# A fused DFT and GEGLU kernel: value matmuls in two accumulating passes, channel 128 through DRAM, last output pieces over all banks

## The chip, the cores and the metric

The kernel runs on one core of a Trainium2 chip. The metric is device time in microseconds (us), measured over repeated executions. Before: 684.08 us, median of 4 runs (683.23 to 684.66).

Engines: PE is the tensor engine, PEld its weight loads (they bring in the stationary operand, the matrix that stays in PE while the other streams past; they overlap its matmuls), DVE is VectorE, ACT is ScalarE, POOL is GpSimd, SP issues DMAs.

## The reference, cut to what matters

```python
X = np.fft.fft(np.fft.fft(x, axis=1), axis=2).real   # x: 8 x 3008 x 256
g   = X @ w_gate                                     # 256 x 1536
val = X @ w_val                                      # 256 x 1536
out = (gelu(g) * val) @ w_out                        # 1536 x 256, all tokens
```

## The kernel before

The real part of the DFT is symmetric, so the kernel computes half the tokens of each batch entry and splits them into an even part E and an odd part O. A token then has the gate `E@WE + O@WO` (the plus row) and its mirror token `E@WE - O@WO` (the minus row). One batch entry is a *block*, its tokens are three *chunks* of 512, 512 and 481 columns, and each chunk has twelve *units* of 128 hidden columns: 36 units a block, 288 in all. Into the units of a block the DFT of the next block is woven as filler, one small piece a unit: first eight stage-1 steps (every other unit, 16 units long), then channel steps and the E, channel-128 and O steps. The order of instructions is set by a scheduler from these pieces, not by the loop alone.

The gate takes three matmuls: E and O add up in a bank, ScalarE takes the gelu of the plus row, then M = -2·O is added to the same bank for the minus row. The value came in two forms. In 207 units ("apart") E and O were multiplied into two banks and VectorE made both rows; in 81 units a third value matmul (M) made the minus row, as for the gate, and VectorE only multiplied.

```python
def l1_value(ci, fc):                      # before, cut
    if apart(ci, fc):                      # fc % 4 != 3, and not the first chunk of block 0
        mm(pv, n, "v", "E", fs, E, True, True)
        mm(po, n, "v", "M", fs, O, True, True)
        # three VectorE passes: E + channel 128, then plus row, then minus row
        nc.vector.scalar_tensor_tensor(ve, EB_bufs[b][...], w128[...], pv, op0=ALU.mult, op1=ALU.add)
        nc.vector.scalar_tensor_tensor(vv[:, 0, :n], po, -0.5, ve, op0=ALU.mult, op1=ALU.add)
        nc.vector.scalar_tensor_tensor(<vv, reversed>, po, 0.5, ve, op0=ALU.mult, op1=ALU.add)
    else:
        mm(pv, n, "v", "E", fs, E, True, False)
        mm(pv, n, "v", "O", fs, O, False, True)
        nc.vector.tensor_tensor(h[:, fc, 0, :n], gl[:, 0, :n], pv, op=ALU.mult)   # pass 1 of 2
# l1_value2: apart -> GpSimd multiplies both rows of 1024 columns;
#            else  -> matmul with M, and VectorE's pass 2 of 2
...
def s1_pack(j0):                           # one stage-1 step
    s1_mm(j0)                              # two banks: lo, hi
    nc.scalar.activation(up8, hi, AF.Copy)
    for g, op in enumerate((ALU.add, ALU.subtract)):
        nc.vector.tensor_tensor(dst_g, lo, up8, op=op)       # two VectorE passes of 384
...
def b_pack(gi):                            # channel 128 on all partitions
    for off, k2, n in cols[gi]:            # 8 matmuls, one column of Z repeated 128 times
        nc.tensor.matmul(ps[:, off:off+n], _sub(Z, [[0, 128]], k2*C + 128), TPI[:, 0:n], ...)
    nc.scalar.activation(EB[...], ps[:, :n], AF.Copy)
```

PSUM, the memory that PE writes its sums into, has eight banks: two for the gate, three for the value, one for the output, two for the transforms.

## Time and profile before

| what | before |
|---|---|
| time | 684.08 us |
| PE / DVE / ACT / POOL busy | 652.0 / 580.4 / 484.7 / 459.9 of 681.9 us |
| period of a steady block | 79.08 us |
| block 0, from its first unit | 82.87 us |

I take stage times from the trace as the start of the weight load of each unit's WvE matrix (288 of them); a block is from its first such load to that of the next block. Only differences between kernels are read from them.

First the page of the kernel before: busy time, share of the span and instructions of each engine, then the chain of waits by engine, then three groups of instructions (busy us, mean ns of one, idle time before and what ended it).

```profile
PE 652.0 (96%) x5257; PEld 443.7 (65%) x5313; DVE 580.4 (85%) x958; ACT 484.7 (71%) x943; POOL 459.9 (67%) x264
...
PE 81%; DVE 2%; ACT 2%; issue 1%; POOL 1%; DMA 1%; SPq 0%; ACTq 0%; DVEq 0%
...
L543 DVE SCALAR_TENSOR_TENSOR ve_sb<-EB_sb,w,ps_v 128x512 f32<-128x512 bf16 (+1 forms) x207 | 150.5, 732 | 46.0 <-PE ps_v L510 45.6
L549 DVE SCALAR_TENSOR_TENSOR v_sb<-ps_v,ve_sb 128x512 f32<-128x512 f32 (+1 forms) x207 | 138.7, 670 | 0.0
L555 DVE TENSOR_TENSOR h_sb<-gelu_sb,ps_v 128x512 bf16<-128x512 bf16 (+1 forms) x81 | 54.5, 674 | 9.6 <-PE ps_v L510 7.6
```

PE is the limit over the whole span. But an average hides stages. The windows view of the kernel before gives for each stretch its length and then the busy time of each engine: the first chunk of block 0; the VectorE-heavy stretch after it; the stage-1 stretch of block 5 (its first 16 units); the rest of that block. They are cut at the WvE loads. (The prediction quotes windows cut up to 3 us later: in 434.5 to 470 VectorE is busy for 35.0 of 35.5 us.)

```profile
core 0: us, PE busy (x) PEld busy (x) DVE busy (x) ACT busy (x) POOL busy (x), PEclk, DMA share, GB/s
32.20:56.40 24.20, 24.04 (x168) 12.34 (x170) 22.40 (x36) 20.60 (x40) 0.00 (x0) 1.00 0.74 145
56.40:85.00 28.60, 28.13 (x211) 17.96 (x214) 27.99 (x50) 20.02 (x39) 16.55 (x9) 1.00 0.17 34
431.60:466.20 34.60, 34.33 (x271) 23.64 (x275) 33.73 (x58) 23.34 (x47) 23.48 (x12) 1.00 0.17 39
466.20:510.60 44.40, 44.29 (x385) 30.80 (x386) 35.98 (x58) 35.76 (x70) 33.10 (x17) 1.00 0.19 42
```

In the stage-1 stretch VectorE has almost no room left (33.73 of 34.60); after it there are eight free microseconds (35.98 of 44.40).

What one VectorE pass costs is read from starts, not from durations, since listed durations overlap. The timeline of VectorE before (start us, duration us, engine, line, operation):

```profile
440.41 0.68 DVE L555 TENSOR_TENSOR h_sb<-gelu_sb,ps_v 128x512 bf16<-128x512 bf16 x1
441.00 0.74 DVE L543 SCALAR_TENSOR_TENSOR ve_sb<-EB_sb,w,ps_v 128x512 f32<-128x512 bf16 x1
441.67 0.69 DVE L583 TENSOR_TENSOR h_sb<-gelu_sb,ps_v 128x512 bf16<-128x512 bf16 x1
442.27 0.68 DVE L547 SCALAR_TENSOR_TENSOR v_sb<-ps_v,ve_sb 128x512 f32<-128x512 f32 x1
442.87 0.68 DVE L549 SCALAR_TENSOR_TENSOR v_sb<-ps_v,ve_sb 128x512 f32<-128x512 f32 x1
```

A product takes the engine for 0.59 to 0.60 us (440.41 to 441.00, 441.67 to 442.27), a sum or difference for 0.60 (442.27 to 442.87), the E pass for 0.67 (441.00 to 441.67).

### The profile page before, as it was taken

The page shows a single profiled execution, that of the slowest core. Times are in us where ns is not written, and L with a number is a line of the kernel's source. Part 1 is how long each engine was busy: PE and PEld are TensorE (multiplying, and loading weights), DVE is VectorE, ACT ScalarE, POOL GpSimd, SP SyncE. Part 2 cuts the span into 40 slices and gives each one's busy share as a digit, 9 for nine tenths or more (in the row PEclk, how much of TensorE's full clock was granted, in tenths as well). Part 3 has the DMA queues.
Part 4 walks back from the last instruction along what each step waited for, and adds up shares of the span by engine and source line. Part 5 has one row for each costly group of instructions (what it writes and reads, how often), then busy time and mean ns, then how long its engine had stood idle before and what let it go on. Part 6 is the DMA issues. An engine that isn't in the chain of part 4 may idle for free.

```text
span 681.9 us, 14383 instructions
## 1 busy us (share of the span) xinstructions
PE 652.0 (96%) x5257; PEld 443.7 (65%) x5313; DVE 580.4 (85%) x958; ACT 484.7 (71%) x943; POOL 459.9 (67%) x264
## 2 busy tenths in 40 slices
PE   2799999999999999999999999999999999999995
PEld 1555666666766667666776666666666666666664
DVE  8699986998789978999779988899779987788870
ACT  4587687668876688767876688767886678766650
POOL 8303675777776877678767776777776777687770
PEclk9999999999999999999999999999999999999999
DMA  9780251144111611216111441211212111121212
GB/s 248 168 184 16 40 123 40 34 83 89 40 43 38 131 42 39 47 36 131 37 43 40 87 86 33 48 40 36 47 34 47 32 44 43 36 48 44 46 45 62
DMA packets 36278, 43.44 MB, mean 64 GB/s; under 512 B 6668, under 2 KB 33292, under 8 KB 34700
## 3 DMA queue, kind: packets, MB, share of 16 engines
q1 hardware_dynamic: 32432, 30.47, 18.4%
q0 software_dynamic: 3184, 11.57, 9.7%
q8 instruction: 41, 0.67, 0.4%
q10 hardware_dynamic: 592, 0.49, 0.3%
q14 instruction: 29, 0.24, 0.1%
HBM read 29.43 MB, written 24.64 MB: 79 GB/s over the span
## 4 chain that ended last, share of the span: by engine, by line
PE 81%; DVE 2%; ACT 2%; issue 1%; POOL 1%; DMA 1%; SPq 0%; ACTq 0%; DVEq 0%
PE ps_o L603 33%; PE ps_g L510 23%; PE ps_v L510 18%; PE ps_dft L413 3%; PE ps_dft L365 2%; POOL h_sb L580 1%; DMA out_dram<-out_sb 1%; DVE v_sb L547 1%; PE ps_dft L448 1%; PE ps_dft L460 1%; PE ps_dft L435 1%; DVE v_sb L549 0%; ACT gelu_sb L568 0%; DVE ve_sb L543 0%; ACT out_sb L623 0%
## 5 line engine op out<-in xcount | busy, mean ns | idle before, releaser
L580 POOL TENSOR_TENSOR h_sb<-gelu_sb,v_sb 128x1024 bf16<-128x1024 bf16 (+1 forms) x207 | 433.4, 2104 | 193.0 <-ACT gelu_sb L568 122.5
L603 PE MATMUL ps_o<-Wo_sb,h_sb 128*128 128x256 bf16 (+1 forms) x2304 | 308.9, 272 | 4.2 <-DVE out_sb L616 2.1
L525 ACT ACTIVATE gelu_sb<-ps_g 128x512 bf16<-128x512 f32 (+1 forms) x288 | 169.4, 588 | 134.1 <-PE ps_g L510 106.0
L603 PEld LDWEIGHTS <-h_sb 128*128 128x128 bf16 (+1 forms) x2304 | 218.5, 100 | 52.7 <-issue 6.4
L543 DVE SCALAR_TENSOR_TENSOR ve_sb<-EB_sb,w,ps_v 128x512 f32<-128x512 bf16 (+1 forms) x207 | 150.5, 732 | 46.0 <-PE ps_v L510 45.6
L568 ACT ACTIVATE gelu_sb<-ps_g 128x512 bf16<-128x512 f32 (+1 forms) x288 | 168.2, 584 | 2.4 <-PE ps_g L510 2.4
L547 DVE SCALAR_TENSOR_TENSOR v_sb<-ps_v,ve_sb 128x512 f32<-128x512 f32 (+1 forms) x207 | 140.0, 676 | 12.9 <-PE ps_v L510 0.5
L549 DVE SCALAR_TENSOR_TENSOR v_sb<-ps_v,ve_sb 128x512 f32<-128x512 f32 (+1 forms) x207 | 138.7, 670 | 0.0
L510 PE MATMUL ps_g<-EO_sb,WgM 128*128 128x512 bf16 (+1 forms) x288 | 108.3, 376 | 2.3
L510 PE MATMUL ps_v<-EO_sb,WvE 128*128 128x512 bf16 (+1 forms) x288 | 108.2, 376 | 0.4
L510 PE MATMUL ps_g<-EO_sb,WgE 128*128 128x512 bf16 (+1 forms) x286 | 107.2, 375 | 0.2 <-ACT gelu_sb L568 0.2
L510 PE MATMUL ps_v<-EO_sb,WvM 128*128 128x512 bf16 (+1 forms) x288 | 103.9, 376 | 0.6 <-DVE h_sb L555 0.2
L510 PE MATMUL ps_g<-EO_sb,WgO 128*128 128x512 bf16 (+1 forms) x235 | 88.4, 376 | 0.1
L623 ACT ACTIVATE out_sb<-ps_o 128x512 f32<-128x512 f32 x92 | 54.6, 593 | 23.9 <-PE ps_o L603 21.5
L555 DVE TENSOR_TENSOR h_sb<-gelu_sb,ps_v 128x512 bf16<-128x512 bf16 (+1 forms) x81 | 54.5, 674 | 9.6 <-PE ps_v L510 7.6
L583 DVE TENSOR_TENSOR h_sb<-gelu_sb,ps_v 128x512 bf16<-128x512 bf16 (+1 forms) x81 | 54.7, 676 | 7.6 <-PE ps_v L510 3.7
L393 DVE TENSOR_TENSOR A_sb<-ps_dft,up_sb 128x384 bf16<-128x384 f32 x112 | 57.4, 549 | 0.0
L365 PEld LDWEIGHTS <-x_sb 94*128 94x128 bf16 x512 | 32.0, 101 | 34.8 <-DVE x_sb L237 19.0
L420 ACT ACTIVATE Z_sb<-ps_dft 128x512 bf16<-128x512 f32 x88 | 52.5, 601 | 0.2 <-PE ps_dft L413 0.2
L510 PEld LDWEIGHTS <-WvE 128*128 128x128 bf16 x288 | 28.2, 98 | 32.0 <-issue 0.5
L510 PEld LDWEIGHTS <-WgM 128*128 128x128 bf16 x288 | 28.2, 98 | 29.5
L510 PEld LDWEIGHTS <-WvM 128*128 128x128 bf16 x288 | 28.1, 98 | 24.8 <-issue 0.7
(101 smaller groups left out, 443.5 us busy)
## 6 DMA issues: line engine op xcount, KB each, us to landing
out_dram<-out_sb SPq DMA_DIRECT2D x361, 64.0 KB, 2.0
x_sb<-in_x_dram POOLq DMA_DIRECT2D x14, 752.0 KB, 8.0
x_plain<-in_x_dram SPq DMA_DIRECT2D x4, 384.0 KB, 7.4
x_plain<-in_x_dram SPq DMA_DIRECT2D x2, 768.0 KB, 7.4
Wo_sb<-in_moe_w_out_dram POOLq DMA_DIRECT2D x2, 384.0 KB, 6.6
wg_hi<-in_moe_w_gate_dram SPq DMA_DIRECT2D x2, 256.0 KB, 4.0
wv_hi<-in_moe_w_val_dram SPq DMA_DIRECT2D x2, 256.0 KB
wg_lo<-in_moe_w_gate_dram SPq DMA_DIRECT2D x2, 256.0 KB, 4.8
```

Source lines behind the costliest of these rows:

```text
L393: nc.vector.tensor_tensor(dst, lo, up8, op=op)
L510: nc.tensor.matmul(ps[:, :n], W[nm, part][:, fs], src, start=start, stop=stop, **kw)
L525: nc.scalar.activation(gl[:, 0, :n], pg[:, :n], AF.Gelu)
L543: nc.vector.scalar_tensor_tensor(ve[:, :n], EB_bufs[b][:, c0 : c0 + n], w128[:, fc : fc + 1], pv[:, :n], op0=ALU.mult, op1=ALU.add)
L547: nc.vector.scalar_tensor_tensor(vv[:, 0, :n], po[:, :n], -0.5, ve[:, :n], op0=ALU.mult, op1=ALU.add)
L549: nc.vector.scalar_tensor_tensor(_sub(vv, [[-1, n]], TOK + n - 1), po[:, :n], 0.5, ve[:, :n], op0=ALU.mult, op1=ALU.add)
L555: nc.vector.tensor_tensor(st["h"][:, fc, 0, :n], gl[:, 0, :n], pv[:, :n], op=ALU.mult)
L568: nc.scalar.activation(dst, pg[:, :n], AF.Gelu)
L580: nc.gpsimd.tensor_tensor(st["h"][:, fc, :, :n], gl[:, :, :n], pv[:, :, :n], op=ALU.mult)
L583: nc.vector.tensor_tensor(_sub(st["h"], [[-1, n]], (fc * 2 + 1) * TOK + n - 1), gl[:, 1, :n], pv[:, :n], op=ALU.mult)
L603: nc.tensor.matmul(pso[:m, sign, :], st["h"][:, fc, sign, h0 : h0 + m], Wo_sb[:, fc, :], start=(fc == 0), stop=(fc == NFC - 1),)
L623: nc.scalar.activation(osb[:m], pso[:m], AF.Copy)
```

## The change

The intent: five matmuls in every unit instead of six in 81 of them. E and O accumulate in one bank, with VectorE copying the E part out between the two; the plus row is the finished bank, the minus row is twice the copied E part minus the bank. Channel 128 is computed once, as a few narrow matmuls whose stationary operand is 8, 7 or 1 columns wide, sent to DRAM and read back on all partitions. The eight last output pieces take turns over all eight banks. The copied E part and the minus row get three buffers each instead of two. The order of steps in a unit changes from `GgVvfLL` to `GgVLvLf` (G, g: first and second part of the gate; V, v: of the value; L: an output piece; f: filler).

```diff
@@ b_pack, blocks after 0
-                for off, k2, n in cols[gi]:                    # 24 matmuls a block, 128 columns each
-                    nc.tensor.matmul(ps[:, off:off+n], _sub(Z, [[0, 128]], k2*C + 128), TPI[:, 0:n], ...)
-                nc.scalar.activation(EB[...], ps[:, :n], AF.Copy)
+                for i, (off, k2, nk, w) in enumerate(runs):    # 4 matmuls a block, nk = 8, 8, 7, 1
+                    nc.tensor.matmul(ps[:nk, i*K1 : i*K1+w], _sub(Z, [[C, nk]], k2*C + 128), TPI[:, 0:w], ...)
+                    nc.vector.tensor_copy(e128[:nk, :w], ps[:nk, i*K1 : i*K1+w])
+                    nc.sync.dma_start(out=<row128 in DRAM>, in_=e128[:nk, :w])
+                nc.sync.dma_start(out=EB[...], in_=<row128, read on 128 partitions>)
... (o_pack: partition 0 of O by DMA instead of ScalarE)
@@ value, all units
+                mm(pv, n, "v", "E", fs, E, True, True)
+                nc.vector.scalar_tensor_tensor(ve, EB[...], w128[...], pv, op0=ALU.mult, op1=ALU.add)
... (l1_value2, one step later)
+                mm(pv, n, "v", "O", fs, O, False, True, skip_group_check=True)
+                nc.vector.tensor_tensor(h[:, fc, 0, :n], gl[:, 0, :n], pv, op=ALU.mult)
+                nc.vector.scalar_tensor_tensor(<vv, reversed>, ve, 2.0, pv, op0=ALU.mult, op1=ALU.subtract)
+                nc.gpsimd.tensor_tensor(h[:, fc, 1, :n], gl[:, 1, :n], vv, op=ALU.mult)
@@ l2_piece, last chunk
+                        tag, nb = (("o", 1), ("g", 2), ("v", 3), ("dft", 2))[(2 * sub + sign) % 4]
@@
-    SLOT = "GgVvfLL"
+    SLOT = "GgVLvLf"
```

More of the change, by code (lines that the diff above doesn't have):

```diff
@@ L90 @@
     for nm in ("g", "v"):
-        for part in ("E", "O", "M"):
+        for part in ("E", "O", "M") if nm == "g" else ("E", "O"):
             W[nm, part] = const_pool.tile([128, F], BF16, name=f"W{nm}{part}")
@@ L111, in EB_tile, with e128_tile @@
         return work_pool.tile([128, HALF], BF16, tag="EB", bufs=2, name="EB_sb")
+    def e128_tile():
+        return work_pool.tile([8, K1], BF16, tag="e128", bufs=2, name="e128_sb")
     def gelu_tile():
@@ L119, in ve_tile @@
     def ve_tile():
-        return work_pool.tile([128, TOK], FP32, tag="ve", bufs=2, name="ve_sb")
+        return work_pool.tile([128, TOK], FP32, tag="ve", bufs=3, name="ve_sb")
     def v_tile():
-        return work_pool.tile([128, 2, TOK], FP32, tag="v", bufs=2, name="v_sb")
+        return work_pool.tile([128, TOK], FP32, tag="v", bufs=3, name="v_sb")
     def osb_tile():
@@ L138, in ps_dft @@
         return psum_pool.tile([128, 512], FP32, tag="dft", bufs=2, name="ps_dft")
+    dram_pool = ctx.enter_context(tc.tile_pool(name="dram", bufs=1, space=bass.MemoryType.DRAM))
+    row128 = [dram_pool.tile([1, HALF], BF16, name=f"row128_{i}")[:, :] for i in range(2)]
     x_tiles = []
@@ L178 @@
     rd = work_pool.tile([128, 2 * NPH], FP32, tag="Z", bufs=1, name="rd")
-    small = work_pool.tile([128, 4, C], FP32, tag="v", bufs=2, name="small")
-    fp, rp, dc, off = (small[:, i, :] for i in range(4))
+    fp, rp, dc, off = (
+        work_pool.tile([128, C], FP32, tag=t, bufs=3, name=f"small_{i}")[:, :]
+        for i, t in enumerate(("v", "v", "ve", "ve")))
     dt_ = const_pool.tile([128, 2 * K1], FP32)
@@ L336, in run @@
                 W[nm, "O"][:, fs], lo, keep, ps[:, :n], op0=ALU.mult, op1=ALU.subtract)
-            nc.scalar.activation(W[nm, "M"][:, fs], W[nm, "O"][:, fs], AF.Copy, scale=keep2)
+            if nm == "g":
+                nc.scalar.activation(W[nm, "M"][:, fs], W[nm, "O"][:, fs], AF.Copy, scale=keep2)
         return run
@@ L446, in run @@
                 ps = st["ps_b"] = ps_dft()
-                for off, k2, n in cols[gi]:
+                n = chunk_len[gi]
+                if b == 0:
+                    for off, k2, w in cols[gi]:
+                        nc.tensor.matmul(
+                            ps[:, off : off + w], _sub(st["Z"], [[0, 128]], k2 * C + 128), TPI[:, 0:w],
+                            start=True, stop=True)
+                    nc.scalar.activation(_sub(st["EB"], [[1, n]], chunk_off[gi]), ps[:, :n], AF.Copy)
+                    return
+                runs = []
+                for off, k2, w in cols[gi]:
+                    if runs and runs[-1][1] + runs[-1][2] == k2 and w == K1:
+                        runs[-1][2] += 1
+                    else:
+                        runs.append([off, k2, 1, w])
+                dst = row128[b % 2]
+                for i, (off, k2, nk, w) in enumerate(runs):
                     nc.tensor.matmul(
-                        ps[:, off : off + n], _sub(st["Z"], [[0, 128]], k2 * C + 128), TPI[:, 0:n],
+                        ps[:nk, i * K1 : i * K1 + w], _sub(st["Z"], [[C, nk]], k2 * C + 128), TPI[:, 0:w],
                         start=True, stop=True)
-                n = chunk_len[gi]
-                nc.scalar.activation(_sub(st["EB"], [[1, n]], chunk_off[gi]), ps[:, :n], AF.Copy)
+                    e128 = e128_tile()
+                    nc.vector.tensor_copy(e128[:nk, :w], ps[:nk, i * K1 : i * K1 + w])
+                    o = chunk_off[gi] + off
+                    nc.sync.dma_start(
+                        out=ap_replace(dst, ap=[[w, nk], [1, w]], offset=dst.offset + o), in_=e128[:nk, :w])
+                nc.sync.dma_start(
+                    out=_sub(st["EB"], [[1, n]], chunk_off[gi]),
+                    in_=ap_replace(dst, ap=[[0, 128], [1, n]], offset=dst.offset + chunk_off[gi]))
             return run
@@ L464, in run @@
                 nc.scalar.activation(_sub(EO, [[1, n]], off), ps[:, :n], AF.Copy)
-                nc.scalar.activation(
-                    _sub(EO, [[1, n]], off, part_num=1), _sub(st["ps_b"], [[1, n]], 0, part_num=1), AF.Copy)
+                if b == 0:
+                    nc.scalar.activation(
+                        _sub(EO, [[1, n]], off, part_num=1), _sub(st["ps_b"], [[1, n]], 0, part_num=1), AF.Copy)
+                else:
+                    dst = row128[b % 2]
+                    nc.sync.dma_start(
+                        out=_sub(EO, [[1, n]], off, part_num=1),
+                        in_=ap_replace(dst, ap=[[0, 1], [1, n]], offset=dst.offset + chunk_off[gi]))
             return run
@@ L501, in ffn_work, with cols_of @@
         cstate = {}
-        def apart(ci, fc):
-            return fc % 4 != 3 and (b, ci) != (0, 0)
         def mm(ps, n, nm, part, fs, src, start, stop, **kw):
             nc.tensor.matmul(ps[:, :n], W[nm, part][:, fs], src, start=start, stop=stop, **kw)
+        def cols_of(ci, fc):
+            n, c0 = chunk_len[ci], chunk_off[ci]
+            E, O = (EO_bufs[b][:, i, c0 : c0 + n] for i in range(2))
+            if ci not in cstate:
+                cstate[ci] = {"h": h_tile(), "ps": {}, "pso": {}}
+            return n, c0, E, O, cstate[ci], slice(fc * 128, (fc + 1) * 128)
         def l1_gate(ci, fc):
             def run():
-                n = chunk_len[ci]
-                c0 = chunk_off[ci]
-                E, O = (EO_bufs[b][:, i, c0 : c0 + n] for i in range(2))
-                if ci not in cstate:
-                    cstate[ci] = {"h": h_tile(), "ps": {}, "pso": {}}
-                st = cstate[ci]
-                fs = slice(fc * 128, (fc + 1) * 128)
+                n, _, E, O, st, fs = cols_of(ci, fc)
                 pg = ps_g()
@@ L525, in run, with l1_gate2 @@
                 nc.scalar.activation(gl[:, 0, :n], pg[:, :n], AF.Gelu)
-                st["ps"][fc] = [pg, gl, None]
+                st["ps"][fc] = [pg, gl]
+            return run
+        def l1_gate2(ci, fc):
+            def run():
+                n, _, _, O, st, fs = cols_of(ci, fc)
+                pg, gl = st["ps"][fc][:2]
+                mm(pg, n, "g", "M", fs, O, False, True, skip_group_check=True)
+                nc.scalar.activation(_sub(gl, [[-1, n]], TOK + n - 1), pg[:, :n], AF.Gelu)
             return run
@@ L530, in run @@
             def run():
-                n = chunk_len[ci]
-                c0 = chunk_off[ci]
-                E, O = (EO_bufs[b][:, i, c0 : c0 + n] for i in range(2))
-                st = cstate[ci]
-                fs = slice(fc * 128, (fc + 1) * 128)
-                gl = st["ps"][fc][1]
-                pv = ps_v()
-                if apart(ci, fc):
-                    mm(pv, n, "v", "E", fs, E, True, True)
-                    po = ps_v()
-                    mm(po, n, "v", "M", fs, O, True, True)
-                    ve = ve_tile()
-                    nc.vector.scalar_tensor_tensor(
-                        ve[:, :n], EB_bufs[b][:, c0 : c0 + n], w128[:, fc : fc + 1], pv[:, :n],
-                        op0=ALU.mult, op1=ALU.add)
-                    vv = v_tile()
-                    nc.vector.scalar_tensor_tensor(
-                        vv[:, 0, :n], po[:, :n], -0.5, ve[:, :n], op0=ALU.mult, op1=ALU.add)
-                    nc.vector.scalar_tensor_tensor(
-                        _sub(vv, [[-1, n]], TOK + n - 1), po[:, :n], 0.5, ve[:, :n], op0=ALU.mult, op1=ALU.add)
-                    st["ps"][fc][2] = vv
-                else:
-                    mm(pv, n, "v", "E", fs, E, True, False)
-                    mm(pv, n, "v", "O", fs, O, False, True)
-                    nc.vector.tensor_tensor(st["h"][:, fc, 0, :n], gl[:, 0, :n], pv[:, :n], op=ALU.mult)
-                    st["ps"][fc][2] = pv
-            return run
-        def l1_gate2(ci, fc):
-            def run():
-                n = chunk_len[ci]
-                c0 = chunk_off[ci]
-                O = EO_bufs[b][:, 1, c0 : c0 + n]
-                fs = slice(fc * 128, (fc + 1) * 128)
-                pg, gl, _ = cstate[ci]["ps"][fc]
-                mm(pg, n, "g", "M", fs, O, False, True, skip_group_check=True)
-                dst = _sub(gl, [[-1, n]], TOK + n - 1) if apart(ci, fc) else gl[:, 1, :n]
-                nc.scalar.activation(dst, pg[:, :n], AF.Gelu)
+                n, c0, E, _, st, fs = cols_of(ci, fc)
+                pv = ps_v()
+                mm(pv, n, "v", "E", fs, E, True, True)
+                ve = ve_tile()
+                nc.vector.scalar_tensor_tensor(
+                    ve[:, :n], EB_bufs[b][:, c0 : c0 + n], w128[:, fc : fc + 1], pv[:, :n],
+                    op0=ALU.mult, op1=ALU.add)
+                st["ps"][fc] += [pv, ve]
             return run
@@ L572, in run @@
             def run():
-                n = chunk_len[ci]
-                c0 = chunk_off[ci]
-                O = EO_bufs[b][:, 1, c0 : c0 + n]
-                st = cstate[ci]
-                fs = slice(fc * 128, (fc + 1) * 128)
-                _, gl, pv = st["ps"].pop(fc)
-                if apart(ci, fc):
-                    nc.gpsimd.tensor_tensor(st["h"][:, fc, :, :n], gl[:, :, :n], pv[:, :, :n], op=ALU.mult)
-                else:
-                    mm(pv, n, "v", "M", fs, O, False, True, skip_group_check=True)
-                    nc.vector.tensor_tensor(
-                        _sub(st["h"], [[-1, n]], (fc * 2 + 1) * TOK + n - 1),
-                        gl[:, 1, :n], pv[:, :n], op=ALU.mult)
+                n, _, _, O, st, fs = cols_of(ci, fc)
+                _, gl, pv, ve = st["ps"].pop(fc)
+                mm(pv, n, "v", "O", fs, O, False, True, skip_group_check=True)
+                nc.vector.tensor_tensor(st["h"][:, fc, 0, :n], gl[:, 0, :n], pv[:, :n], op=ALU.mult)
+                vv = v_tile()
+                nc.vector.scalar_tensor_tensor(
+                    _sub(vv, [[-1, n]], n - 1), ve[:, :n], 2.0, pv[:, :n], op0=ALU.mult, op1=ALU.subtract)
+                nc.gpsimd.tensor_tensor(st["h"][:, fc, 1, :n], gl[:, 1, :n], vv[:, :n], op=ALU.mult)
             return run
@@ L598, in run @@
                 h0 = n - sub * 128 - m if sign else sub * 128
-                if (sign, f0) == (0, 0):
-                    st["pso"][sub] = ps_o()
-                pso = st["pso"][sub]
+                if last(ci):
+                    if f0 == 0:
+                        tag, nb = (("o", 1), ("g", 2), ("v", 3), ("dft", 2))[(2 * sub + sign) % 4]
+                        st["pso"][sub, sign] = psum_pool.tile(
+                            [128, 2, C], FP32, tag=tag, bufs=nb, name=f"ps_{tag}")
+                    pso = st["pso"][sub, sign]
+                else:
+                    if (sign, f0) == (0, 0):
+                        st["pso"][sub] = ps_o()
+                    pso = st["pso"][sub]
                 for fc in range(f0, f0 + L2P):
```

## The prediction

> **What bounds it now.** TensorE: 652.0 of 681.9 us busy on the page, granted clock 1.000, and 81% of the chain of waits is PE. A block repeats every 79.1 us (four equal blocks in the chain, from 348.46 to 586.01). Starts in the PE timeline: a 512-column matmul every 0.2155 us, a 481-column one every 0.205, eight of 256 columns in 0.875, eight of 64 in 0.235. But a block has two stages. In the windows view, 434.5 to 470 us, where the stage-1 transforms of the next block are woven in, VectorE is busy 35.0 of 35.5 us and waits only 0.2 us, so it already runs at the limit together with PE; from 470 to 511 us it is busy 32.4 of 41.3. Block 0 from 54.4 to 86.5 us is VectorE-bound too (31.4 of 32.1).
>
> **Removed from PE.** 81 of 288 units lose their sixth value matmul: about 17 us. In seven blocks the channel-128 broadcast needs four small matmuls instead of 24: about 0.5 us a block, 3.7 us in all. Sum about 20.6 us; in a steady block 9 x 0.21 + 0.5 = 2.4 us (79.1 to 76.7). ScalarE loses the EB and one-partition copies (about 1.1 us for each of 21 groups), GpSimd goes from 207 operations of 2.1 us to 288 of about half; neither is the limit.
>
> **Added to VectorE.** Every unit now takes three passes over PSUM: start to start 0.66 (E part), 0.60 (product), 0.60 (difference), so 1.87 us for 512 columns, 1.77 for 481. The Trainium skill ("VectorE: DVE Perf Modes", the perf-mode tier table) holds a tensor_tensor with a PSUM operand at 1x; the 0.60 us starts for 512 elements agree, so none gets cheaper. Units that took two passes (81) pay about 0.66 us more; the others only lose bubbles of about 0.2 us between the E pass and its reader. Per steady block VectorE needs 66.1 + 7.4 (stage 1) + 0.6 (row copies) = 74 us, under PE's 76.7, but not in each stage:
> - stage-1 stretch, 16 units: VectorE 1.87 + 0.465 = 2.33 us a unit (2.21 now), PE 2.13: 3.1 us short, of which three value banks let PE run ahead by perhaps 1.9;
> - the other 20 units: PE-bound, 2.16 or 2.10 against 1.87 or 1.77.
> So a steady block gains about 2.4 - 1.2 = 1.2 us.
>
> **Block 0.** Its first chunk, all two-pass, shares VectorE with the weight folds (20.5 of 22.1 us busy); twelve extra passes add 8 us, about 2 hidden in gaps. The next, VectorE-bound stretch adds 2, the last chunk returns 1: net +7.
>
> **Tail.** Eight last output pieces, 1.47 us each, with gaps of about 0.5 us waiting for the one bank: the new banks close them, but output buffers and stores (about 3.6 us a cycle, two buffers) then limit: -1.5.
>
> **Sum.** 683.65 + 7 - 6 x 1.2 - 1.9 (block 7, no filler) - 1.5 = 680; I shade it to **678 us, 8 in 10 between 666 and 691**. Faster by over 2%: 0.2; within 2%: 0.72; slower: 0.08.
>
> **What would show it.** PE busy falls about 20 us but the span far less; VectorE above 92% of the span, nearly without waits in stage-1 windows; new PE waits on VectorE's E pass or value banks there; block period 77 to 78.5 us; first chunk of block 0 ends some 5 us later; GpSimd near 300 us.
>
> **What would make it wrong.** VectorE passes starting closer than I read, or a reordered schedule that lets PE run farther ahead: then the full 20 us shows (about 662). Or row writes and read-backs on the store queue, about 2 us each, holding stores, output buffers and the one output bank: slower.

## The result, and the profile after

683.02 us, median of 4 runs (681.82 to 683.29), against 684.08 us: the ratio is 0.9992, with a 95% interval of 0.9973 to 1.0011. That is no change. Later experiments were each timed beside runs of the kernel before on one chip; the changed kernel itself was not run again, so I compare ratios. The interval of each ratio is about 0.0015 to 0.002 to either side, so two ratios that differ by less than about 0.0025 (1.7 us, an estimate from these intervals) are not told apart by time alone.

The page of the changed kernel (the same parts as above; L575 is the E pass, L588 the difference, L586 the product):

```profile
PE 643.4 (94%) x5038; PEld 432.2 (63%) x5092; DVE 631.2 (93%) x1067; ACT 468.0 (69%) x897; POOL 356.0 (52%) x345
...
PE 82%; ACT 6%; DVE 4%; DMA 3%; issue 1%; SPq 0%; POOL 0%; ACTq 0%; DVEq 0%; POOLq 0%
...
L575 DVE SCALAR_TENSOR_TENSOR ve_sb<-EB_sb,w,ps_v 128x512 f32<-128x512 bf16 (+1 forms) x288 | 209.8, 731 | 9.4 <-PE ps_v L541 8.8
L586 DVE TENSOR_TENSOR h_sb<-gelu_sb,ps_v 128x512 bf16<-128x512 bf16 (+1 forms) x288 | 194.0, 674 | 12.0 <-ACT gelu_sb L557 5.2
L588 DVE SCALAR_TENSOR_TENSOR v_sb<-ve_sb,ps_v 128x512 f32<-128x512 f32 (+1 forms) x288 | 192.5, 668 | 0.0
```

PE has 8.6 us less busy time, VectorE 50.8 more, and VectorE's idle time before the E pass fell from 46.0 to 9.4 us: its room is gone. The windows of the same stretches, without the second one (first chunk of block 0, stage-1 stretch of block 5, rest of block 5):

```profile
32.20:63.30 31.10, 25.89 (x166) 12.09 (x167) 29.96 (x48) 22.13 (x41) 11.97 (x11) 1.00 0.57 111
436.10:472.20 36.10, 35.59 (x279) 24.56 (x284) 35.54 (x63) 24.30 (x47) 18.19 (x16) 1.00 0.20 45
472.20:514.50 42.30, 42.15 (x349) 28.48 (x349) 39.66 (x67) 32.89 (x64) 23.01 (x21) 1.00 0.20 46
```

In the first row PE is busy for only 25.89 of 31.10 us while VectorE is busy for 29.96: that chunk has changed its limit (before, PE was busy for 24.04 of 24.20). Worked out from the starts of the WvE loads:

| stretch | before | after | difference | predicted |
|---|---|---|---|---|
| block 0 | 82.87 | 89.25 | +6.4 | +7 |
| blocks 1 to 6 together | 474.8 | 471.5 | -3.3 | -7.2 |
| block 7 and tail | 92.21 | 88.38 | -3.8 | -3.4 |
| steady block (block 5 after) | 79.08 | 78.42 | -0.66 | -1.2 |

The loss in block 0 and the gain at the end are close to what was predicted. For block 0 that is partly luck: its first chunk lost 6.8 us (24.42 to 31.18) where 6 were reckoned, and the rest gained 0.4 where a loss of 1 was. The steady block gained half.

Where did the steady block lose it? In its trace I subtracted from every start the streaming time of the matmul before. Apart from a few matmuls whose records are missing, the changed kernel has two kinds of small holes that the kernel before has not. Six are of 0.09 to 0.25 us: five in the stage-1 stretch and just after it, one where the last chunk begins, 1.07 us in all. (When I wrote the expectations below I had counted only the five, 0.86 us.) The others are 0.1 us before and 0.1 us after each narrow channel-128 matmul, about 0.8 us a block. The timeline of the changed kernel around one of these:

```profile
484.62 0.10 PEld L541 LDWEIGHTS <-WvE 128*128 128x128 bf16 x1
484.72 0.38 PE L541 MATMUL ps_v<-EO_sb,WvE 128*128 128x512 bf16 x1
485.03 0.09 PEld L470 LDWEIGHTS <-Z_sb 128*8 128x8 bf16 x1 [0.32 <-issue]
485.03 0.20 PE L470 MATMUL ps_dft<-TPI,Z_sb 128*8 128x64 bf16 x1
485.16 0.10 PEld L541 LDWEIGHTS <-WgE 128*128 128x128 bf16 x1
485.17 0.39 PE L541 MATMUL ps_g<-EO_sb,WgE 128*128 128x512 bf16 x1
```

A 512-column matmul lets the next one start 0.2155 us later, so the narrow one should start at 484.94. It starts at 485.03, and its weight load only there too, where other weight loads run under the matmul before them. From WvE to WgE 0.45 us pass, so the narrow matmul, 64 columns long, costs 0.45 - 0.2155 = 0.23 us. Four a block cost about 0.9 us. The 24 wide matmuls that they replaced had cost 0.70 us, as this timeline of the kernel before shows (eight of them in 429.60 to 429.83):

```profile
429.60 0.39 PE L448 MATMUL ps_dft<-TPI,Z_sb 128*128 128x64 bf16 x8
429.83 0.38 PE L460 MATMUL ps_dft<-TPI,Z_sb 128*128 128x64 bf16 x8
```

So my theory after the result (A) had three separate losses: VectorE in block 0, VectorE in the stage-1 stretch, and narrow matmuls that PE can't overlap. The rivals: VectorE sets the block alone, so PE holes cost nothing; or the stage-1 stretch is held by transform banks, by the order of steps or by the store queue; or block 0's loss comes from the new order of steps.

### The profile page after: what moved, and what is told of

It is laid out like the page before. It is cut to its first block, busy times and chain, and to the rows that moved or that the text cites. A ratio compares the mean times of both kernels' runs of the same rounds, so it can differ in the third digit from the quotient of the medians.

```text
span 681.3 us, 14441 instructions
## 1 busy us (share of the span) xinstructions
PE 643.4 (94%) x5038; PEld 432.2 (63%) x5092; DVE 631.2 (93%) x1067; ACT 468.0 (69%) x897; POOL 356.0 (52%) x345
## 4 chain that ended last, share of the span: by engine, by line
PE 82%; ACT 6%; DVE 4%; DMA 3%; issue 1%; SPq 0%; POOL 0%; ACTq 0%; DVEq 0%; POOLq 0%
PE ps_o L615 35%; PE ps_g L541 24%; PE ps_v L541 16%; DMA out_dram<-out_sb 3%; PE ps_dft L420 3%; PE ps_dft L372 2%; ACT gelu_sb L566 2%; DVE x_sb L243 2%; ACT gelu_sb L557 1%; ACT out_sb L635 1%; PE ps_dft L488 1%; PE ps_dft L442 1%; ACT Z_sb L427 1%; PE ps_g L338 1%; ACT EO_sb L492 1%
## 5 line engine op out<-in xcount | busy, mean ns | idle before, releaser
L590 POOL TENSOR_TENSOR h_sb<-gelu_sb,v_sb 128x512 bf16<-128x512 bf16 (+1 forms) x288 | 329.8, 1145 | 289.3 <-DVE v_sb L588 200.7
L615 PE MATMUL ps_o<-Wo_sb,h_sb 128*128 128x256 bf16 (+1 forms) x2232 | 341.8, 272 | 3.0 <-ACT gelu_sb L566 1.1
L615 PEld LDWEIGHTS <-h_sb 128*128 128x128 bf16 (+1 forms) x2304 | 228.6, 100 | 108.8 <-issue 3.3
L575 DVE SCALAR_TENSOR_TENSOR ve_sb<-EB_sb,w,ps_v 128x512 f32<-128x512 bf16 (+1 forms) x288 | 209.8, 731 | 9.4 <-PE ps_v L541 8.8
L586 DVE TENSOR_TENSOR h_sb<-gelu_sb,ps_v 128x512 bf16<-128x512 bf16 (+1 forms) x288 | 194.0, 674 | 12.0 <-ACT gelu_sb L557 5.2
L588 DVE SCALAR_TENSOR_TENSOR v_sb<-ve_sb,ps_v 128x512 f32<-128x512 f32 (+1 forms) x288 | 192.5, 668 | 0.0
L541 PE MATMUL ps_v<-EO_sb,WvO 128*128 128x512 bf16 (+1 forms) x288 | 108.2, 376 | 0.6
L397 ACT ACTIVATE up_sb<-ps_dft 128x384 f32<-128x384 f32 x56 | 27.5, 490 | 21.3 <-PE ps_dft L372 21.3
L420 PE MATMUL ps_dft<-CS,A_sb 128*128 128x128 bf16 x372 | 40.5, 222 | 1.2 <-ACT Z_sb L427 0.6
L372 PE MATMUL ps_dft<-G,x_sb 94*128 94x96 bf16 x468 | 35.6, 208 | 4.7 <-DVE x_sb L243 4.6
```

The costliest lines, as they stand in the source:

```text
L372: nc.tensor.matmul(ps[:, jj * 96 : (jj + 1) * 96], xt[:, j0 + jj, cc * 128 : (cc + 1) * 128], G[:, j0 + jj, :], start=True, stop=True,)
L420: nc.tensor.matmul(ps[:, o : o + 128], A[:, g, k2 + d, :], CS[:, g, :], start=True, stop=True)
L541: nc.tensor.matmul(ps[:, :n], W[nm, part][:, fs], src, start=start, stop=stop, **kw)
L575: nc.vector.scalar_tensor_tensor(ve[:, :n], EB_bufs[b][:, c0 : c0 + n], w128[:, fc : fc + 1], pv[:, :n], op0=ALU.mult, op1=ALU.add)
L586: nc.vector.tensor_tensor(st["h"][:, fc, 0, :n], gl[:, 0, :n], pv[:, :n], op=ALU.mult)
L588: nc.vector.scalar_tensor_tensor(_sub(vv, [[-1, n]], n - 1), ve[:, :n], 2.0, pv[:, :n], op0=ALU.mult, op1=ALU.subtract)
```

## The experiments

All are edits of the changed kernel, except the control. Eleven kernels ran, all results correct but the one made wrong on purpose.

### Wide stationary operand for the row matmuls

```diff
-    ps[:nk, ...], _sub(st["Z"], [[C, nk]], k2 * C + 128)
+    step, m = (C // 16, 16 * nk - 15) if nk > 1 else (0, 128)   # every 16th column is a wanted one
+    ps[:m, ...],  _sub(st["Z"], [[step, m]], k2 * C + 128)
... (copy of m rows; the DMA takes every 16th partition)
```

> The changed kernel, but the 28 small channel-128 matmuls load 97 to 128 stationary columns (every sixteenth one is wanted) instead of 8, 7 or 1; the same rows go to DRAM, results are unchanged. Theory A (a narrow stationary operand is loaded only when the matmul before it has ended, so each of the 28 costs about 0.23 us of PE time instead of 0.03): the gaps around them vanish, 28 x 0.2 = 5.6 us, most of it real because they lie in the PE-bound part of a block; 677.5 to 679.5 us, block period from 78.5 to about 77.8. Rival (VectorE sets the block period anyway): within 1 us of the changed kernel, 682 to 684.

Measured: 679.48 us, ratio to before 0.9943 (0.9929 to 0.9958), so about 3.3 us less than the changed kernel (0.9992). The period of block 5 went from 78.42 to 77.84. The trace of this kernel, for the same place:

```profile
483.20 0.38 PE L544 MATMUL ps_v<-EO_sb,WvE 128*128 128x512 bf16 x1
483.20 0.29 PEld L471 LDWEIGHTS <-Z_sb 128*113 128x113 bf16 x1
483.42 0.19 PE L471 MATMUL ps_dft<-TPI,Z_sb 128*113 128x64 bf16 x1
483.44 0.38 PE L544 MATMUL ps_g<-EO_sb,WgE 128*128 128x512 bf16 x1
```

WvE to WgE takes 0.24 us instead of 0.45, and the weight load now starts with the matmul before (483.20). PE's weight loads come in the same order as in the changed kernel, in each of blocks 1 to 6, so the gain isn't one of order. It is somewhat less than I wrote down (3.3 us, expected 3.5 to 5.5): in other places 0.1 us remains after the matmul.

### Narrow, with the step of the wide one

```diff
-    _sub(st["Z"], [[C, nk]], k2 * C + 128)
+    _sub(st["Z"], [[C // 16, nk]], k2 * C + 128)     # wrong channels: wrong on purpose
```

> The changed kernel with the row matmuls still 8, 7 and 1 columns wide, but taken with the step of the wide variant (16 elements, not 256). The result is wrong on purpose (wrong channels go into the rows). It separates width from step, which the wide variant changed together. Theory A (the narrow width makes PE wait): the weight loads of the 28 matmuls still find PE's loader idle 0.2 to 0.4 us before them, block period 78.4 to 78.7, 682 to 684 us. Rival (the step of 256 elements is at fault): the gaps go as in the wide variant, period about 77.9, 679 to 680 us.

Measured: 681.93 us, ratio 0.9982 (0.9960 to 1.0004), wrong result as intended (relative error 0.091), block 5 at 78.42, the holes as in the changed kernel. The weight-load groups of the changed kernel, of this one and of the wide one (mean ns, then idle time before):

```profile
L470 PEld LDWEIGHTS <-Z_sb 128*8 128x8 bf16 x14 | 1.3, 91 | 3.4 <-issue 3.4
```

```profile
L470 PEld LDWEIGHTS <-Z_sb 128*8 128x8 bf16 x14 | 1.3, 92 | 3.4 <-issue 3.4
```

```profile
L471 PEld LDWEIGHTS <-Z_sb 128*113 128x113 bf16 x14 | 4.0, 287 | 0.1
```

Width decides, not the step. (The order of PE's weight loads is again that of the changed kernel.) The wide load even takes three times as long, 287 against 91 ns, and costs less, because it runs under the matmul before it. The Trainium skill says in "TensorEngine Tiling (Array Packing)", section Key Properties, "Mode switching requires drain: Changing tiling mode (not just tile) drains the TensorE". A wait of 0.1 us before and 0.1 us after, tied to the width, fits that, but the trace does not show the mode, so that part is argued and not shown.

### The old broadcast back

```diff
-    <four narrow matmuls, VectorE copies, DMAs to DRAM and back>
+    <24 matmuls of 128 equal columns, ScalarE copies to EB and to partition 0 of O>
```

> The changed kernel with channel 128 broadcast as before (24 wide matmuls and ScalarE copies a block, no row to DRAM, no read back). Theory A (28 narrow matmuls cost 0.23 us each, 0.92 us a block, where the 24 wide ones cost 0.705): a block gets 0.2 us shorter on PE and is spared the store queue, but ScalarE takes 3.4 us more a block; 680 to 683 us. Rival, as in the prediction (the row path saves 0.5 us a block): 685 to 688 us.

Measured: 681.95 us, ratio 0.9974 (0.9959 to 0.9988), 1.2 us less than the changed kernel; block 5 at 78.16. So the row path, predicted to save 3.7 us, costs about 1.2. By time alone 1.2 us is not clear of noise, but a saving of 3.7 us is excluded, and the block period agrees (0.26 us less, where the holes gave 0.2).

### The first chunk of block 0 on the six-matmul path

```diff
+    if six(ci):                                  # (b, ci) == (0, 0)
+        mm(pv, n, "v", "E", fs, E, True, False)
+        mm(pv, n, "v", "O", fs, O, False, True)
+        nc.vector.tensor_tensor(h[:, fc, 0, :n], gl[:, 0, :n], pv, op=ALU.mult)
... (and in l1_value2 the matmul with M and the second product, as before)
```

> The changed kernel, but the first chunk of block 0 takes the old six-matmul, two-pass path; all else as changed. Theory A (that chunk is bound by VectorE, where twelve more passes stand beside the weight folds): the first twelve units of block 0 go from 31.2 us back to about 24.5 and the whole to 676 to 678 us. Rival (the 6 us of block 0 come from the new order of steps or are given back in its last chunk): 681 to 684 us.

Measured: 675.62 us, ratio 0.9887 (0.9870 to 0.9904), 7.2 us less than the changed kernel. The first twelve units of block 0 took 24.6 us instead of 31.2. The windows view of this kernel for them:

```profile
32.00:56.60 24.60, 24.44 (x165) 12.15 (x167) 22.17 (x36) 20.44 (x40) 0.00 (x0) 1.00 0.42 79
```

PE is busy for 24.44 of 24.60 us again. This loss is twelve VectorE passes beside the weight folds, and it is not given back later.

### One stage-1 pass on GpSimd, with a second ScalarE copy

GpSimd can't read PSUM (the Trainium skill, "Trainium Kernel Development and Optimization", Key Constraints; no run here tries it), so its operands need copies.

```diff
     nc.scalar.activation(up8, hi, AF.Copy)
+    nc.scalar.activation(lo8, lo, AF.Copy)
     nc.vector.tensor_tensor(dst_0, lo, up8, op=ALU.add)
-    nc.vector.tensor_tensor(dst_1, lo, up8, op=ALU.subtract)
+    nc.gpsimd.tensor_tensor(dst_1, lo8, up8, op=ALU.subtract)
```

> The changed kernel, but of the two VectorE additions of each stage-1 step one is done by GpSimd, from two ScalarE copies. VectorE saves 0.47 us a step, 3.7 us a block, so it needs 2.10 us a unit in the stage-1 stretch where PE needs 2.13. Theory A (VectorE is what makes PE idle there, about 1 us a block, 1.5 to 2 in block 0): first 16 units of a steady block from 36.05 to about 34.5 us, period from 78.5 to 77.3 to 77.7, the whole 674 to 677 us. Rival (the steady block lost its gain to the row matmuls and the store queue alone): period above 78.2, the whole 681 us or more.

Measured: 680.93 us, ratio 0.9968 (0.9954 to 0.9981), block 5 at 78.25: a miss for my theory as written, and on the rival's side by the number. But the trace shows something else than the rival said. The six holes are gone, and three of 0.3 us stand in the block instead, one every 13 us, 0.9 us in all. This kernel's timeline at one of them:

```profile
440.75 0.50 ACT L398 ACTIVATE up_sb<-ps_dft 128x384 f32<-128x384 f32 x1
441.12 0.62 ACT L561 ACTIVATE gelu_sb<-ps_g 128x512 bf16<-128x512 f32 x1
441.59 0.63 ACT L570 ACTIVATE gelu_sb<-ps_g 128x512 bf16<-128x512 f32 x1
441.87 0.10 PEld L545 LDWEIGHTS <-WgE 128*128 128x128 bf16 x1
442.28 0.38 PE L545 MATMUL ps_g<-EO_sb,WgE 128*128 128x512 bf16 x1
```

WgE has its weights at 441.97 and starts at 442.28, just after the gelu that frees its bank ends (441.59 + 0.63 = 442.22). ScalarE had the new copy (L398) in front. This is read from the timeline, so it was a reading to be tested: take the pass from VectorE without loading ScalarE.

### One stage-1 pass on GpSimd, by difference

```diff
-    nc.scalar.activation(up8, hi, AF.Copy)
-    for g, op in enumerate((ALU.add, ALU.subtract)):
-        nc.vector.tensor_tensor(dst_g, lo, up8, op=op)
+    nc.scalar.activation(up8, hi, AF.Copy, scale=2.0)
+    nc.vector.scalar_tensor_tensor(dst_0, up8, 0.5, lo, op0=ALU.mult, op1=ALU.add)
+    nc.gpsimd.tensor_tensor(dst_1, dst_0, up8, op=ALU.subtract)
```

> The changed kernel, but GpSimd makes the second half of each stage-1 step by difference (first half minus twice the copied part, the copy scaled by 2 as it is made), so VectorE loses one of its two 0.47 us passes and ScalarE gets nothing new. Earlier run with a second ScalarE copy: PE's small gaps in 464 to 475 us (0.86 us a block) went, but three gaps of 0.3 us came before gate matmuls that waited for a gelu. Theory A (VectorE costs PE 0.86 us a block, the new ScalarE copy ate that gain): block period from 78.45 to 77.5 to 77.7, whole 676 to 678 us. Rival (some other limit, such as transform banks or the order of steps, holds PE): period 78.2 or more, whole 680 or more.

Measured: 671.72 us, ratio 0.9825 (0.9809 to 0.9841), 11.4 us less than the changed kernel, more than expected. Every steady block takes 77.37 us; the changed kernel's take 78.42 to 78.92, so the edit returns 1.05 us in blocks 5 and 6 and up to 1.55 in others. Block 0 is 4.0 us shorter (85.22). The windows of its block 5:

```profile
425.10:458.80 33.70, 33.32 (x268) 23.30 (x273) 32.86 (x56) 23.08 (x45) 24.74 (x24) 1.00 0.19 45
458.80:502.50 43.70, 43.59 (x361) 29.68 (x361) 40.48 (x66) 33.79 (x66) 23.51 (x22) 1.00 0.20 47
```

The stage-1 stretch fell from 36.1 to 33.7 us, but part of that is work moved out of it: it has 273 weight loads where the changed kernel has 284, and the rest of the block grew from 42.3 to 43.7 us. VectorE is still nearly full there. The six holes are gone; those around the narrow matmuls remain. Against the run with the second ScalarE copy, whose PE order is the same but for one weight load, a block is 0.88 us shorter (78.25 to 77.37): that goes with the extra copy.

One thing is not separated. The edit also gave PE another order. The scheduler set the last two of the eight stage-1 steps 26.5 and 30.8 us after the block's first WvE load; in the changed kernel they come at 26.3 and 27.9, and there the holes begin. Each of the six holes ends when a ScalarE instruction ends, and none when a VectorE pass does: the gate matmul at 464.03 starts after the gelu that ends at 463.98, the stage-1 matmul at 464.42 after the copy that ends at 464.36, the output matmul at 468.68 after the copy that ends at 468.63. Nor does the waits list of the changed kernel for PE, from 120 to 590 us, name VectorE (waited for: us in total, times, longest):

```profile
PE ps_o L615 <- ACT gelu_sb L566: 1.0, 6, 0.2
PE ps_o L615 <- ACT out_sb L635: 0.2, 1, 0.2
```

So it is shown that the edit returns 1.05 us and more a block. That VectorE's passes as such held PE, and not the order that PE got beside them or a transform bank that two VectorE passes kept, is argued; no run changes one without the other.

### Control: the same relief on the kernel before

> The kernel before with the stage-1 half by difference on GpSimd, which gave the changed kernel 11 us. Theory A (before, PE sets the steady block alone and VectorE just keeps up; the relief is worth something only where the change has overloaded VectorE): block period 79.1 as before, block 0 up to 3 us shorter, whole 680 to 684 us. Rival (the relief is a gain of its own, whatever the value passes): period 78.2 or less, whole 676 us or less.

Measured: 681.25 us, ratio 0.9961 (0.9946 to 0.9977), steady block 79.14 as before, block 0 shorter by 1.9 us (81.00). So the relief is worth 2.7 us there and 11.4 us in the changed kernel: most of it pays for something that the change brought, the fuller VectorE or the order that came with it.

### Two value banks, three transform banks

```diff
-    tag="v", bufs=3 ...   tag="dft", bufs=2
+    tag="v", bufs=2 ...   tag="dft", bufs=3
```

> The changed kernel with two value banks and three transform banks instead of three and two. Theory A, as in the prediction (three value banks let PE run ahead of VectorE in the stage-1 stretch): PE waits for value banks there, period above 79.5, whole 690 us or more. Rival (PE's stops in that stretch are on transform banks, and value banks have room): period below 78.3, whole 682 us or less.

Measured: 699.08 us, ratio 1.0227 (1.0212 to 1.0243), 16 us slower than the changed kernel, blocks of 80.0 to 81.0 us. The third value bank can't be spared: PE now waits for the E pass (4.2 us in six waits, `PE ps_v <- DVE ve_sb` in its waits list), which it never does in the changed kernel's list. So the value banks do carry the run-ahead of PE over VectorE. Whether a third transform bank would help if no value bank paid for it is not shown.

### The tail on one bank again

```diff
-    tag, nb = (("o", 1), ("g", 2), ("v", 3), ("dft", 2))[(2 * sub + sign) % 4]
+    st["pso"][sub] = ps_o()
```

> The changed kernel with the last output pieces on the one output bank again, as before. Theory A (the banks close seven gaps of 0.5 us on PE, but two output buffers and the stores then set the pace): 684 to 685 us, 1 to 2 us slower than the changed kernel. Rival (the tail was already paced by the stores alone): equal within 0.5 us, 682.5 to 683.5.

Measured: 684.39 us, ratio 1.0017 (1.0003 to 1.0030), 1.7 us slower than the changed kernel by ratio, at the edge of the noise; the trace agrees, with 90.2 us for block 7 and tail against 88.4. The banks do gain, and the timeline of the changed kernel shows why not more: PE starts its last piece at 672.16, but the copies wait for stores.

```profile
672.16 1.47 PE L615 MATMUL ps_g<-Wo_sb,h_sb 128*128 128x256 bf16 x12
674.04 0.38 ACT L631 ACTIVATE out_sb<-ps_dft 128x256 f32<-128x256 f32 x1 [2.76 <-DMA out_dram<-out_sb]
674.38 0.42 DVE L628 COPY out_sb<-ps_o 128x256 f32<-128x256 f32 x1 [2.70 <-DMA out_dram<-out_sb]
677.16 0.38 ACT L631 ACTIVATE out_sb<-ps_g 128x256 f32<-128x256 f32 x1 [2.74 <-DMA out_dram<-out_sb]
```

### The mends together

First chunk on six matmuls, wide row matmuls and the stage-1 half by difference:

> The changed kernel with three mends: first chunk of block 0 on the six-matmul path (measured alone: -7.4 us), wide stationary operand for the row matmuls (-3.5 us alone), second stage-1 half by difference on GpSimd. Theory A (three separate losses in different stretches, which add up): 683.0 - 7.4 - 3.5 - 5.5, so 665 to 668 us, faster than the kernel before by over 2%. Rival (they share one limit and do not add): 672 us or more.

Measured: 661.90 us, ratio 0.9685 (0.9671 to 0.9699). The single gains were 7.2 + 3.3 + 11.4 = 21.9 us; together 0.9992 - 0.9685 of 684 us is 21.0. They add within the noise, so they are separate losses. A steady block takes 76.90 us. (Block 0 takes 79.58 us here and 78.59 in the next run, with the same code for it, so the time of its first chunk is good to about 1 us; the rest of it is 54.44 us in both.)

Then eight buffers for the last pieces:

```diff
-    osb = osb_tile()                                   # two buffers
+    tag, nb = (("osb", 2), ("v", 3), ("ve", 3))[(2 * sub + sign) % 3]
+    osb = work_pool.tile([128, 2, C], FP32, tag=tag, bufs=nb, name="last_sb")
```

> The three mends together (661.9 us) and, for the eight last output pieces, eight buffers (two of the output, three each of the value tiles, idle by then) instead of two. In the changed kernel PE has issued its last piece 3 us before the last copy, and each copy waits 2.7 to 3.8 us for a store. Theory A (two buffers and their stores pace the tail since the banks were spread): the copies follow PE every 1.3 us, 3 to 4 us less, 658 to 659 us. Rival (the stores themselves, issued in turn on two queues, pace it): within 1 us of 661.9.

Measured: 659.34 us, ratio 0.9644 (0.9624 to 0.9665), 2.8 us less by ratio (0.9685 - 0.9644 of 684), where 3 to 4 were expected. In its timeline the last copy starts 1.5 us after PE starts the last piece, where it was 5.0:

```profile
649.79 1.47 PE L633 MATMUL ps_g<-Wo_sb,h_sb 128*128 128x256 bf16 x12
650.06 0.42 DVE L647 COPY last_sb<-ps_o 128x256 f32<-128x256 f32 x1 [2.26 <-PE ps_o L633]
651.30 0.38 ACT L650 ACTIVATE last_sb<-ps_g 128x256 f32<-128x256 f32 x1 [2.24 <-PE ps_g L633]
```

This version beats both kernels: 3.6% faster than before.

## Why the prediction was right or wrong

The prediction said 678 us and a gain; the measured time, 683.02 us, is inside its range, but there was no gain clear of noise. The step that failed is the saving by the channel-128 matmuls; its miss of 0.7 us a block accounts for what the steady blocks failed to gain (3.9 us in blocks 1 to 6). The bookkeeping of the steady block, with measured terms, closes: 79.08 - 1.91 (nine matmuls: six of 0.2155, three of 0.205 us) + 0.2 (row path) = 77.37 us, which is the period with the stage-1 half by difference; the 1.05 us that this edit returned make it 78.42, the period of the changed kernel.

- **"81 of 288 units lose their sixth value matmul: about 17 us."** Right on PE; it is the 1.91 us of a steady block.
- **"the channel-128 broadcast needs four small matmuls instead of 24: about 0.5 us a block, 3.7 us in all."** This step failed. I costed a small matmul by its streaming time, from wide ones in a row (0.235 us for eight). The narrow ones cost 0.23 us each. In place of a saving of 0.5 us a block there is a cost of 0.2, and in place of -3.7 us the undo shows +1.2: 4.9 us of the sum. That is 0.7 us a block, which covers the difference between the steady block predicted (-1.2) and measured (-0.66).
- **"16 units: VectorE 1.87 + 0.465 = 2.33 us a unit ... 3.1 us short, of which three value banks let PE run ahead by perhaps 1.9 ... a steady block gains about 2.4 - 1.2"**. Right in place and nearly in size: what the relief returned is 1.05 us in blocks 5 and 6, up to 1.55 in others, and the bank experiment shows that PE needs the third value bank. The mechanism is shown only in part: the forecast "new PE waits on VectorE's E pass or value banks there" did not come true. The holes end with ScalarE instructions, and the edit that removed them also changed PE's order.
- **Block 0, "net +7"**: +6.4 in the trace (first chunk +6.8, rest -0.4); the undo of its first chunk alone returned 7.2 us.
- **Tail, "-1.5"**: the undo showed 1.7, and the reason given (two buffers, then stores) was tested with eight buffers and held.
- **"PE busy falls about 20 us but the span far less; VectorE above 92% of the span"**: PE fell by 8.6 us only: a listed 512-column matmul lasts 0.38 us while the next starts after 0.2155, so a short hole still counts as busy. VectorE is at 93%. **"block period 77 to 78.5"**: 78.42 to 78.92, partly outside. **GpSimd "near 300 us"** is 356, with 1145 ns for one product where I had halved 2104.
- **"I shade it to 678 us"**: the sum was 680 and nothing measured stood behind the two microseconds. With the failed term as measured the sum is 680 + 4.9 = 685, against 683.

The warning that row writes and read-backs could hold the store queue did not come true in any size that matters. Blocks 1 to 4 of the changed kernel take 78.57 to 78.92 us against 78.42 in blocks 5 and 6 (before: 79.07 to 79.08, once 79.41), and four waits of a ScalarE copy on the read-back, 3.4 us in all, are in the waits list; but similar variation stays with the old broadcast (78.16 to 79.07). PE's order in blocks 1 to 4 differs from that in 5 and 6, and the largest extra hole (0.35 us, in block 3) ends with a ScalarE output copy that had waited 0.81 us for an output store. With the stage-1 half by difference the variation is gone. What starts it is left open.

## What to carry to other kernels

When a change moves work from the engine that is busiest on average to another, cost it stage by stage: here 1.9 us a block came off PE, but the stage-1 stretch and the first chunk had no room on VectorE, and a spare engine (GpSimd) paid in full only in a form that put no new copy on ScalarE. When an edit is meant to relieve one engine, compare also the order of instructions: the scheduler may have changed it. Cost a small instruction between large ones by the start-to-start time of the neighbours around it, not by its columns: here a matmul with few stationary columns cost eight times its streaming time (0.23 us against 0.03). If an expected gain is missing, relieve one suspect at a time and then all together; gains that add show separate losses.

## What the Trainium skill lacked or had wrong

- "TensorEngine Tiling (Array Packing)" says that a change of tiling mode drains the engine, but gives no cost and doesn't say whether an ordinary matmul with few stationary columns meets it. Here one of 8, 7 or 1 columns between 128-column ones cost about 0.1 us before and 0.1 us after, whatever its step.
- "TensorE: Matmul & The Clock Gate", LDWEIGHTS, gives the columns over 1.2 as the load time in ns. Estimated by it, 128 columns take 107 ns, and the trace has 98; 113 columns (with a step of 16 elements) take 94 ns, and the trace has 287; 8 columns take 7, and the trace has 91. The page's section on weight-path modes ties a fast load to exactly 128 weights. The wide run's trace agrees (97 columns side by side take 125 ns, 128 take 98) and shows that the step counts too: 97 columns with a step of 16 elements take 256 ns. The formula allows for neither.
- "VectorE: DVE Perf Modes", the perf-mode tier table, holds a tensor_tensor with a PSUM operand at 1x; the traces agree (0.60 us from start to start for 512 columns; at the page's 0.96 GHz the columns alone would be 0.53 us, an estimate). Its section on the drain reports that a semaphore after each of eight copies costs nothing extra, and has no number for a pass that waits for the one just before it; in the kernel before, a pass that reads what the E pass just before it wrote starts 0.87 us after it (391.00 to 391.87, the E pass named as what it waited for), where the one in the timeline above that does not read it starts after 0.67 (441.00 to 441.67).
- "GPSIMD Engine Reference" states a floor of about 2.5 cycles an element at 1.2 GHz for two inputs, which would make 512 columns 1067 ns (an estimate). The runs show, for one bf16 and one fp32 input, 1163 ns for 512 columns, 919 for 384 and 2143 for 1024: 1.91 ns an element ((2143 - 1163) / 512, or 2.3 cycles, under the floor) and about 0.18 us for each instruction, which the page's floor leaves out. (With two fp32 inputs 384 columns took 999 ns.) So half of a long one, as the prediction took it, is too little.
